# Moving PSUM copies between two activations of a group, and one more rest for a batch's first expert block

## The chip, the cores and the metric

The kernel runs on one core of one Trainium2 chip. The metric is the device time of one execution in microseconds (us), the median of several runs. Before the change it is 1380.28 us (three runs, 1379.79 to 1381.28).

The engines have these names: PE is TensorE (matmuls, and PEld its weight loads), DVE is VectorE, ACT is ScalarE, POOL is GpSimd, and SP issues most of the transfers. Each engine takes its instructions in its own order and waits on semaphores for the others. On PE, ACT and DVE this kernel fixes that order in the program: the order in which the Python code calls the instructions is the order on the engine.

## What is computed

Attention in which each query keeps only its 32 best keys, and then a mixture-of-experts layer in which each token goes to one of eight experts:

```python
# q, k, v: (8 batches, 8 heads, 576 positions, 64)
scores = q @ k.T / sqrt(64)
kth    = the 32nd largest score of each row
attn   = softmax(where(scores >= kth, scores, -1e9)) @ v
x      = attn laid out as (4608 tokens, 512)

logits = x @ w_gate                      # 8 experts
expert = argmax(logits);  gate_w = softmax(logits)[expert]
h      = relu(x @ w1[expert])            # 512 -> 1024
out    = gate_w * (h @ w2[expert])       # 1024 -> 512
```

All of it is float32.

## The kernel before

The attention runs in 144 groups, 18 for each of the 8 batches. A group is two tiles of 128 query rows by 576 scores. Two heads share one unit of the program ("head pair"; 4 per batch, 32 in all). For each group:

- PE multiplies queries and keys (`sc`), four groups ahead; ACT copies the scores to SBUF (`s`);
- DVE folds the scores (`h`, `l`, `few`, `hl`) and finds the 32nd largest in four rounds (`tops`);
- ACT computes `low` from it and then two Relus, one for each tile, which mark how far a score lies under the threshold (`w`); POOL subtracts them from the scores; ACT takes the exponentials;
- PE transposes the weights of the group before (`wTm`, `wTl`), ACT copies them out of PSUM (`wT`, `wTt`);
- when a head pair is complete, PE multiplies with the values (`po`, in two halves), ACT copies the two halves (`oT`), PE turns them to rows and multiplies with the gate (`px`, in two parts), ACT copies both parts (`xl`), and POOL divides by the softmax sums.

The loop over the groups, cut to what the change concerns. `at_place(name)` lets the work at a head pair's end go one step on, if it waits at that name:

```python
for i, (b, g) in enumerate(work):
    f_of[i + 1] = fold(s_of[i + 1])                    # DVE
    low, nbias, doubts = search(tiles, s_of[i], ...)   # DVE, then low on ACT
    at_place("small")
    w_of[i] = depths(s_of[i], low)                     # ACT: two Relus
    less(s_of.pop(i), w_of[i])                         # POOL: two subtractions
    doubts()
    ...
    at_place("pool")
    at_place("relu")                                   # ACT: oT or xl copies
    at_place("rows")                                   # POOL: rows of x
    ...
    s_of[i + AHEAD], steps = scores(...)               # ACT: two copies of s
    for step in steps: step()
    evacuate()                                         # ACT: copies due for expert blocks
    at_place("turn")
    turns = turning(i - 1)
    next(turns, None)                                  # PE: wTm, ACT: wT
    rest = pieces(part)                                # PE: pieces of an expert block
    next(turns, None)                                  # PE: wTl
    rest = pieces(now - now//2 - part + rest)          # PE: pieces
    weights(tiles, w_of[i], nbias)                     # ACT: two exponentials
    next(turns, None)                                  # ACT: wTt
    evacuate()                                         # ACT: copies due for expert blocks
    multiply(i + AHEAD + 1)                            # PE: sc
    ...
    at_place("products")                               # PE: po or px
    at_place("weights")
    credit = min(credit + pieces(now//2 + rest), ...)  # PE: pieces
```

```python
def depths(s, low):
    w = ...
    for m in range(2):
        nc.scalar.activation(w[:, m, :], s[:, m], AF.Relu, scale=-STEEP, bias=low[:, m:m + 1])
    return w
```

The end of a head pair is a generator; each `next(out_steps)` gives a matmul part or a copy of `outputs`:

```python
def outputs(n, x):
    for j in range(2):
        ...                                   # PE: po
        yield
        nc.scalar.copy(oT[...], po[...])      # ACT
        yield
    ...                                       # PE: px, two parts
    yield
    for to, px in put:
        nc.scalar.copy(to, px)                # ACT: xl, two parts
```

All PSUM tiles of transposes and of `po` and `px` share one pool of two buffers (`bank`), so a new one waits until the copy of the one before last has been made. The score tiles and the tiles of the expert blocks have two buffers each in pools of their own.

The expert blocks (40 of 128 tokens, over loaded weights) are cut into 16 pieces each and laid between the groups by a credit that the program works out when it is built; those that are left over run after the last group. A piece is four matmuls of `ph` (128x128x128) or one of `py`. A block turns its rows first (`xtp`), ACT copies them (`xTs`), and `ph` multiplies them. Usually the block before turns the rows of the next in good time; a batch's first block has to do it itself:

```python
def evacuate(upto=None):
    while due and (upto is None or upto in [kind for kind, _ in due]):
        due.pop(0)[1]()

def block(n, ...):
    if not hasattr(n, "xT"):
        turned(n)                  # PE: xtp; the ACT copy to xTs becomes due
        yield "pause"              # no more pieces at this place of the group
    evacuate("xT")                 # ACT: all copies due, up to xTs
    ...                            # PE: ph, ...
```

Of the kernel before, what the change touches and what calls it, by code (L numbers as in the profile page):

```python
# [35 lines left out]
def kernel(  # L36
# [326 lines left out]

        return low, nbias, doubts

    def depths(s, low):

        w = k.att.tile([P, 2, S], F32, name="w", bufs=1 if k.exact else 3)
        for m in range(2):
            nc.scalar.activation(  # L370
                w[:, m, :], s[:, m, :, :].rearrange("p j k -> p (j k)"), AF.Relu,
                scale=-STEEP, bias=low[:, m:m + 1],
            )
        return w

    def less(s, w):
# [44 lines left out]
    def outputs(n, x):  # L421

        odd = n.u % 2
        oT = oT_of[odd]
        for j in range(2):
            q = slice(j * HF + (0 if odd else ST), (j + 1) * HF + (0 if odd else ST))
            po = bank("po")
            for c in range(NC):
                for h in range(2):
                    r = slice(h * D, (h + 1) * D)  # L430
                    nc.tensor.matmul(po[r, 0:HF], n.v[:, c, r], wT[:, c, h, q], start=(c == 0), stop=False)  # L431
            nc.tensor.matmul(po[:, 0:HF], n.v[:, NC, :], wTt[:, q], start=False, stop=True)
            yield
            nc.scalar.copy(oT[:, j * HF:(j + 1) * HF], po[:, 0:HF])
            yield
        starts = [t * P + (ST if odd else 0) for t in range(NC)] + [0 if odd else SM]
        xw = P + lw
        n.xl = k.small.tile([P, KC, xw], F32, name="xl", bufs=1)
        put = []
        for t0, t1 in ((0, KC - 2), (KC - 2, KC)):  # L440
            px = bank("px")
            for t in range(t0, t1):
                nc.tensor.matmul(
                    px[:, (t - t0) * xw:(t - t0 + 1) * xw], oT[:, starts[t]:starts[t] + P],
                    turn[:, n.u // 2, odd * lw:odd * lw + xw], start=True, stop=True,
                )
            put.append((n.xl[:, t0:t1, :], px[:, 0:(t1 - t0) * xw].rearrange("p (t w) -> p t w", w=xw)))
        yield
        for to, px in put:
            nc.scalar.copy(to, px)  # L450

    def divisors(n):
        rz = rz_of[n.u % 2]
# [215 lines left out]
# [5 lines that stand above are left out]
    def block(n, following=lambda: None, put_off=lambda store: store()):  # L674

        if not hasattr(n, "xT"):
            turned(n)
            yield "pause"
        evacuate("xT")
        hT = k.mlp.tile([P, FT, P], F32, name="hT", bufs=1)  # L680
        for half in range(2):
            while half and "y" in [kind for kind, _ in due]:
                yield "pause"
            ph = k.ps_m.tile([P, FT // 2, P], F32, name="ph", tag="m")
            for f in range(FT // 2):
                fc = half * (FT // 2) + f
                for dt in range(DT):
                    nc.tensor.matmul(  # L688
                        ph[:, f, :], n.w1[:, 0, dt, fc * P:(fc + 1) * P], n.xT[:, dt, :],
                        start=(dt == 0), stop=(dt == DT - 1),  # L690
                    )
                if f == FT // 2 - 1:
                    due.append((f"h{half}", lambda ph=ph, half=half: nc.scalar.activation(  # L693
                        hT[:, half * (FT // 2):(half + 1) * (FT // 2), :], ph, AF.Relu
                    )))
                yield
        evacuate("h0")
        following()
        yield "pause"
        evacuate()  # L700
        py = bank("py") if k.apart else k.ps_m.tile([P, Dm], F32, name="py", tag="m")
        for f in range(FT):
            nc.tensor.matmul(py, hT[:, f, :], n.w2[:, 0, f, :], start=(f == 0), stop=(f == FT - 1))  # L703
            if f < FT - 1:
                yield
        y = k.mlp.tile([P, Dm], F32, name="y")

        def store():
            put = nc.gpsimd.indirect_dma_start(  # L709
                out=out[:, :], out_offset=bass.IndirectOffsetOnAxis(ap=n.x[:, 0, Dm + 1:XW].bitcast(I32), axis=0),  # L710
                in_=y[:, :], in_offset=None, bounds_check=N - 1, oob_is_err=False,
            )
            if not k.exact:
                tc.add_manual_dep(put.ins, k.last_pool.name, AFTER)

        def scaled():
            nc.scalar.activation(y, py, AF.Copy, scale=n.x[:, 0, Dm:Dm + 1])  # L717
            put_off(store)

        due.append(("y", scaled))  # L720
        yield "last"
# [13 lines left out]
    with fast:  # L735
# [68 lines left out]
        def ending(b, u):  # L804

            nonlocal left
            n = unit[b * U + u]
            if u == 0:
                x_of[b] = k.xp.tile([P, KC, XW], F32, name="x")
                in_turn(token_ids(x_of[b][:, :, Dm + 1].bitcast(I32), b))  # L810
                lg_of[b] = k.small.tile([P, KC, E], F32, name="lg")
            x, lg = x_of[b], lg_of[b]
            out_steps = outputs(n, x)
            yield "products"
            next(out_steps)
            if u % 2 == 0:
                yield "relu"
                next(out_steps)
            yield "small"
            div = divisors(n)  # L820
            aside.append(div)
            if u % 2:
                yield "relu"
                next(out_steps)
            yield "products"
            next(out_steps)
            if b * U + u + 2 < len(units):
                load_values(unit[b * U + u + 2])
            yield "relu"
            next(out_steps)  # L830
            yield "products"
            next(out_steps)
            yield "relu"
            next(out_steps, None)
            yield "rows"
            through(div)
            logits(n, lg)
            rows(n, x)
            if u < U - 1:
                return  # L840
            yield "small"
            r = choice(lg)
            aside.append(r.steps)
            yield "weights"
            yield "turn"
            through(r.steps)
            nc.scalar.activation(lg, lg, AF.Exp)
            yield "products"
            ranks(r)
            yield "small"  # L850
            steps = places(r, x)
            aside.append(steps)
            yield "relu"
            nc.scalar.copy(run, r.run)
            yield "pool"
            through(steps)
            scatters.extend(scattering(r, x))
            if b == B - 1:
                scatter(KC)
                slot_i = k.small.tile([1, 2, NSLOT], I32, name="slot_i")  # L860
                through(table(slot_i, SURE, False))
                firsts = [(slot_i[0:1, 0, j:j + 1], slot_i[0:1, 1, j:j + 1]) for j in range(SURE)]
                ready = load_rows(SimpleNamespace(), firsts[0][1], True)
            new = LAST - SURE if b == B - 1 else new_of[b]
            if new:
                slot_i = slot_last if b == B - 1 else k.small.tile([1, 2, NSLOT], I32, name="slot_i")
                steps = table(slot_i, new, b == B - 1)
                aside.append(steps)
                yield "weights"
                yield "pool"  # L870
                yield "weights"
                yield "pool"
                through(steps)
                coming.extend((slot_i[0:1, 0, j:j + 1], slot_i[0:1, 1, j:j + 1]) for j in range(new))
            if b == B - 1:
                spare.extend(coming[ALWAYS - SURE:])
                del coming[ALWAYS - SURE:]
                assert len(loaded) == 2 and not waiting
                fill_up()
                coming[0:0] = [(firsts[0][0], ready)] + [(expert, (piece,)) for expert, piece in firsts[1:]]  # L880
                scatter(0)
# [10 lines left out]
        got_of, s_of, f_of, w_of = {}, {}, {}, {}  # L892
# [16 lines left out]
        def loop():  # L909
# [9 lines left out]
            for i, (b, g) in enumerate(work):  # L919
# [10 lines left out]
                    then = lambda: fold_on(f_of[i + 1])  # L930
                low, nbias, doubts = search(tiles, s_of[i], f_of.pop(i), then)
                at_place("small")
                w_of[i] = depths(s_of[i], low)
                less(s_of.pop(i), w_of[i])
                doubts()
                put_stores()
                scatter(1)
                at_place("pool")
                at_place("relu")
                at_place("rows")  # L940
                at = i % per_batch
                if at == FIRST and b:
# [180 lines left out]
```

## Time and profile before

| | busy us | share of the span | instructions |
|---|---|---|---|
| PE | 1242.7 | 90% | 7538 |
| DVE | 1097.6 | 80% | 4655 |
| ACT | 919.9 | 67% | 2049 |
| POOL | 649.9 | 47% | 805 |

The span of the profiled execution is 1378.2 us. The page shows the busy share of each engine in 40 slices of 34.5 us; a digit is tenths, and 9 means 90% or more. The row PEclk is the clock that TensorE was granted, in tenths of full speed. A group in the list of groups is named by its line in the program, its engine, its operation and its tiles (out<-in); the mean length of one follows. The groups that the change moves:

| what | count | mean ns |
|---|---|---|
| Relu of one tile (`w<-s,low`, ACT) | 288 | 768 |
| copy of half the outputs (`oT<-po`, ACT) | 64 | 395 |
| copy of a part of the rows (`xl<-px`, ACT) | 64 | 453 |
| copy of a block's turned rows (`xTs<-xtp`, ACT) | 40 | 608 |
| subtraction of one tile (`w<-s,w`, POOL) | 288 | 1434 |

A wait is shown as the idle time of an engine before an instruction, with the instruction that ended it: "ph <- ACT xTs" means that PE stood idle before `ph` until ACT had written `xTs`. A row of the timeline has the start, the length, the engine, the line, the operation, its tiles and how many equal ones were merged; a bracket at its end gives the idle time before it and its releaser. PE counts a float32 matmul as two passes, so its counts there are twice those of the program.

### The profile page before, as it was taken

To read this page: it belongs to the slowest core of one execution; us is meant where nothing else is said; L and a number is where in the kernel's file an instruction comes from. 1 tells how busy PE (TensorE), PEld (TensorE's weight loads), DVE (VectorE), ACT (ScalarE), POOL (GpSimd) and SP (SyncE) were. 2 spreads that over 40 slices of the span, in tenths; PEclk is the share of its full clock that TensorE was granted. 3 is DMA by queue.
4 is the path that set the end of the run, shared out by engine and by line. 5 is a ranking of instruction groups with operands and counts; after the bars stand their busy time and mean duration, and the time that the engine had idled before them with its cause. 6 is when DMAs were issued, how large, how long until landed. Compare 5 with 4: busy or idle time off the path is not lost. (4 is left out here: it accounts for less than half of the span.)

```text
span 1378.2 us, 24231 instructions
## 1 busy us (share of the span) xinstructions
PE 1242.7 (90%) x7538; PEld 847.1 (61%) x7538; DVE 1097.6 (80%) x4655; ACT 919.9 (67%) x2049; POOL 649.9 (47%) x805
## 2 busy tenths in 40 slices
PE   5776777776799999999999999999999999999995
PEld 3444444444466666766766666767676677776773
DVE  8999999999999999999999999999999820000000
ACT  4788777777788888888777788887777821111110
POOL 3454547546645666466555565675556621000000
PEclk9878787888899999999999999999999999999998
DMA  2000011001483267327645474358552859999880
GB/s 82 29 29 29 28 36 55 29 29 36 162 295 127 106 213 277 132 78 247 246 167 173 149 274 161 109 169 302 187 174 66 315 181 354 387 319 330 302 322 18
DMA packets 102219, 231.66 MB, mean 168 GB/s; under 512 B 5182, under 2 KB 25918, under 8 KB 102080
## 3 DMA queue, kind: packets, MB, share of 16 engines
q1 hardware_dynamic: 95328, 209.76, 43.2%
q0 software_dynamic: 6464, 19.97, 4.0%
q8 instruction: 61, 1.00, 0.3%
q14 instruction: 78, 0.64, 0.1%
q10 hardware_dynamic: 288, 0.30, 0.1%
HBM read 208.72 MB, written 22.33 MB: 168 GB/s over the span
## 5 line engine op out<-in xcount | busy, mean ns | idle before, releaser
L379 POOL TENSOR_TENSOR w<-s,w 128x576 f32<-128x576 f32 x288 | 407.2, 1434 | 451.8 <-ACT w L370 451.7
L688 PE MATMUL ph<-xTs,w 128*128 128x128 f32 x2560 | 307.6, 276 | 6.0 <-ACT xTs L665 6.0
L688 PEld LDWEIGHTS ph<-xTs,w 128*128 128x128 f32 x2560 | 298.3, 192 | 23.2 <-issue 14.9
L703 PE MATMUL py<-w,hT 128*128 128x512 f32 x640 | 292.0, 596 | 0.0
L338 DVE MAX8 tops<-scr 128x8 f32<-128x168 f32 x864 | 248.3, 319 | 0.1
L276 PE MATMUL sc<-qkb 64*128 64x288 f32 (+1 forms) x1280 | 224.1, 476 | 9.6 <-ACT s L283 5.2
L387 ACT ACTIVATE w<-w,nbias 128x576 f32<-128x576 f32 x288 | 224.8, 799 | 2.7 <-POOL w L379 2.5
L370 ACT ACTIVATE w<-s,low 128x576 f32<-128x576 f32 x288 | 207.6, 768 | 4.7
L398 PE MATMUL wTm<-turn,w 128*128 128x128 f32 x1152 | 175.2, 291 | 34.5 <-ACT xl L450 21.1
L398 PEld LDWEIGHTS wTm<-turn,w 128*128 128x128 f32 x1152 | 140.2, 149 | 84.0 <-ACT xl L450 23.5
L1002 DVE CAST any_i<-pd 1x1 int32<-1x1 f32 x1 | 0.1, 146 | 236.0 <-PE pd L1000 236.0
L703 PEld LDWEIGHTS py<-w,hT 128*128 128x128 f32 x640 | 114.6, 190 | 116.9 <-issue 115.6
L345 DVE MATCH_REPLACE8 scr<-tops,scr 128x168 f32<-128x168 f32 x576 | 177.9, 314 | 0.0
L283 ACT COPY s<-sc 128x576 f32<-128x576 f32 x288 | 169.9, 645 | 11.3 <-PE sc L276 10.7
L404 ACT COPY wT<-wTm 128x512 f32<-128x512 f32 x256 | 139.9, 609 | 39.4 <-PE wTm L398 39.2
L276 PEld LDWEIGHTS sc<-qkb 64*128 64x128 f32 (+1 forms) x1280 | 119.2, 197 | 73.2 <-issue 26.0
L431 PE MATMUL po<-wT,vb 128*64 128x288 f32 x1024 | 154.8, 450 | 0.4 <-ACT wTt L419 0.4
L709 POOL DMA_INDIRECT out_dram<-y,xg x40 | 40.6, 1015 | 212.1 <-ACT y L717 199.8
L329 DVE MAX8 few<-l 128x8 f32<-128x288 f32 x288 | 128.0, 445 | 0.0
L431 PEld LDWEIGHTS po<-wT,vb 128*64 128x64 f32 x1024 | 74.7, 151 | 77.2 <-issue 26.1
L693 ACT ACTIVATE hT<-ph 128x512 f32<-128x512 f32 x80 | 48.8, 609 | 108.2 <-PE ph L688 108.1
L290 DVE TENSOR_TENSOR h<-s 128x576 f32<-128x576 f32 x144 | 112.5, 781 | 4.4 <-ACT s L283 4.4
(116 smaller groups left out, 1444.0 us busy)
## 6 DMA issues: line engine op xcount, KB each, us to landing
w<-in_moe_w_dram SPq DMA_DIRECT2D x80, 2048.0 KB, 9.8
qkb<-in_qk_dram SPq DMA_DIRECT2D x31, 608.0 KB, 4.2
xg<-x_rows SPq DMA_DIRECT2D x40, 257.0 KB, 9.8
vb<-in_v_dram SPq DMA_DIRECT2D x32, 320.0 KB, 3.2
x_rows<-blank SPq DMA_DIRECT2D x5, 257.0 KB, 13.8
x_rows<-blank POOLq DMA_DIRECT2D x4, 257.0 KB, 8.7
x_rows<-x,posi POOLq DMA_INDIRECT x40, 3.0
out_dram<-y,xg POOLq DMA_INDIRECT x40, 6.1
```

The costliest lines, as they stand in the source:

```text
L276: nc.tensor.matmul(ps[rows, j, 0:HF], n.q[d, cols], n.k[d, keys], start=True, stop=True)
L283: lambda m=m, ps=ps: nc.scalar.copy(s[:, m, :, :], ps[:, :, 0:HF]) for m, ps in enumerate(got)
L338: nc.vector.max(out=tops[:, m, r * 8:(r + 1) * 8], in_=src[m])
L345: nc.vector.match_replace(out=scr[:, m, :], in_to_replace=tops[:, m, r * 8:(r + 1) * 8], in_values=src[m], imm_value=NEG,)
L370: nc.scalar.activation(w[:, m, :], s[:, m, :, :].rearrange("p j k -> p (j k)"), AF.Relu, scale=-STEEP, bias=low[:, m:m + 1],)
L379: k.last_pool = in_turn(nc.gpsimd.tensor_tensor(w[:, m, :], s[:, m, :, :].rearrange("p j k -> p (j k)"), w[:, m, :], op=ALU.subtract)).ins
L387: nc.scalar.activation(w[:, m, :], w[:, m, :], AF.Exp, scale=scale, bias=nbias[:, m:m + 1], accum_out=n.z[:, c:c + 1])
L398: nc.tensor.transpose(pm[:, c * P:(c + 1) * P], w[:, m, first:first + P], ident)
L404: nc.scalar.copy(wT[:, :, m, q], pm4)
L431: nc.tensor.matmul(po[r, 0:HF], n.v[:, c, r], wT[:, c, h, q], start=(c == 0), stop=False)
L688: nc.tensor.matmul(ph[:, f, :], n.w1[:, 0, dt, fc * P:(fc + 1) * P], n.xT[:, dt, :], start=(dt == 0), stop=(dt == DT - 1),)
L703: nc.tensor.matmul(py, hT[:, f, :], n.w2[:, 0, f, :], start=(f == 0), stop=(f == FT - 1))
```

## The change

The copies of `oT` and the first of the two copies of `xl` are made between the two Relus of a group instead of behind both; the second copy of `xl` keeps its place behind them. This is to let the outputs leave PSUM earlier, so that the two shared buffers come free sooner for the transposes that follow, while POOL can begin its first subtraction as before.

A batch's first expert block rests at one place more after its rows were turned, so that it begins only when ScalarE has copied them out of PSUM, and PE goes on with the score products of the group meanwhile.

```diff
-    def depths(s, low):
+    def depths(s, low, between=lambda: None):
         w = ...
         for m in range(2):
             nc.scalar.activation(
                 w[:, m, :], s[:, m, :, :].rearrange("p j k -> p (j k)"), AF.Relu,
                 scale=-STEEP, bias=low[:, m:m + 1],
             )
+            if m == 0:
+                between()
         return w
...
         yield
         for to, px in put:
             nc.scalar.copy(to, px)
+            yield
...
         if not hasattr(n, "xT"):
             turned(n)
             yield "pause"
+            yield "pause"
         evacuate("xT")
...
             next(out_steps)
             yield "relu"
-            next(out_steps, None)
+            next(out_steps)
+            yield "behind"
+            next(out_steps)
             yield "rows"
...
-                w_of[i] = depths(s_of[i], low)
+                w_of[i] = depths(s_of[i], low, lambda: at_place("relu"))
                 less(s_of.pop(i), w_of[i])
                 doubts()
                 put_stores()
                 scatter(1)
                 at_place("pool")
-                at_place("relu")
+                at_place("behind")
                 at_place("rows")
```

## The prediction, before the changed kernel was run

> **What bounds the kernel now.** I read the slices first, because averages over the span mix stages with different limits.
>
> ```profile
> PE   5776777776799999999999999999999999999995
> ...
> DVE  8999999999999999999999999999999820000000
> ...
> PEclk9878787888899999999999999999999999999998
> ```
>
> The reader is to see two borders. VectorE is full from the start to about slice 32; TensorE becomes full at slice 11, 380 us, where the first expert blocks enter between the attention groups, and stays full to the end. Cut at these borders, the table of stretches (us, then busy time of TensorE, weight loads, VectorE, ScalarE, GpSimd) reads:
>
> ```profile
> 0.00:380.00 380.00, 275.95 (x1429) 166.12 (x1430) 372.82 (x1614) 288.34 (x651) 200.97 (x268) 0.83 0.16 50
> 380.00:1110.00 730.00, 714.48 (x4640) 496.09 (x4640) 716.84 (x2996) 588.98 (x1324) 422.14 (x506) 1.00 0.52 187
> 1110.00:1362.00 252.00, 251.40 (x1468) 184.82 (x1468) 7.61 (x43) 41.86 (x74) 25.81 (x30) 1.00 0.84 301
> ```
>
> Until 380 us VectorE's top-32 search is the bound (373 of 380 us; TensorE only 276). From 380 to 1110 us both look full; after that only expert blocks run, and TensorE has 0.6 us idle in 252. Which of the two leads in the middle? VectorE's own waits in the whole attention part are few (4.4 us for the score copies), but its group period is 7.02 us where nothing disturbs it and 7.75 us on average after group 54, though its work per group is the same. TensorE has a fixed list of instructions, and its waits in the window 390 to 1115 us are short:
>
> ```profile
> PE ph L688 <- ACT xTs L665: 5.3, 5, 1.1
> PE wTl L411 <- ACT wT L404: 3.8, 11, 0.7
> PE wTm L398 <- ACT oT L434: 2.9, 3, 1.0
> PE wTm L398 <- ACT xl L450: 1.3, 1, 1.3
> ```
>
> So from 380 us on **TensorE is the bound**: some 966 us busy in 982. I read the time as 380 us of VectorE, then TensorE's list plus its idle time (some 16 us), then 16 us of closing. A VectorE stall after 380 us costs only if TensorE comes to wait for it; I timed the gap between the end of a group's exponentials and the start of its transposes on TensorE, and it never falls under 2.2 us in the groups from 54 to 141. A ScalarE copy counts only if TensorE waits for it.
>
> **What the Trainium skill says.** "PSUM — Partial Sum Buffer", section "Engine vs sequencer instructions", says that ScalarE's queue is strictly first in, first out and that matmuls start in program order. The trace agrees: ScalarE sat idle 44.0 us in 48 waits before the output copies (oT), with the other work queued behind each. "SBUF — State Buffer", section "Who interferes with whom", says that a VectorE instruction with two SBUF inputs and a GpSimd instruction that reads SBUF lock each other out for a whole instruction. The trace agrees: the fold into `few` takes 0.45 us at the median, but 1.51 us when it starts while GpSimd subtracts. These stalls, worked out as what the four fold instructions of each group take over the fastest tenth of their kind, are some 34 us; I take them as the other channel by which a moved Relu can act.
>
> **Part 1: the second Relu behind the output copy.** No instruction is added or removed; the order of the built program shows equal counts on all engines. Four copies per head pair (2 oT of 0.40 us, 2 xl of 0.45 us), 128 in all, stood behind both Relus (1.44 us a pair, so about 0.7 us each). Now oT and the first xl stand between them. Where the matmul is done already, ScalarE's total is the same and the copy comes 0.7 us earlier. Where ScalarE waits for the matmul (48 of 64 oT, 15 xl), the copy cannot come earlier; the second Relu no longer fills the wait, and everything behind it (s, wT, exponentials) slips by the smaller of the wait and 0.67 us.
>
> What slips matters where TensorE waits for the copy of wT: its next transpose (wTl) needs the bank. For each output group after 380 us I took the slip, took off any time that ScalarE waits for TensorE before wT anyway, and compared it with the distance from the end of the first wT copy to the start of wTl. Most have slack of 0.7 to 1.5 us; tight ones have 0.12 or 0.34 us. The positive remainders sum to 4.8 us, of which 1.8 fall in five groups that part 2 also touches (counted there). **Loss: 3.0 us.** Gain: the three waits for oT (2.9 us) lose 0.67 us each, but in those groups wTl follows with a slack of 0.1 us, so nearly all comes back as a wait there; the one xl wait gives perhaps 0.2 us. **Gain: 0.5 us.**
>
> **Part 2: the second rest of a batch's first block.** It touches six places (380, 514, 649, 797, 932, 1080 us). The built order shows it: before, wTl, two or three pieces of ph (8 or 12 matmuls, which the trace counts as 16 or 24 passes), sc; after, wTl, sc, then all of ph. On TensorE and ScalarE before, at 514 us (start, length):
>
> ```profile
> 513.16 0.27 PE L411 MATMUL wTl<-turn,w 128*128 128x128 f32 x1
> 514.49 2.05 PE L688 MATMUL ph<-xTs,w 128*128 128x128 f32 x16 [1.06 <-ACT xTs L665]
> 516.47 1.24 PE L276 MATMUL sc<-qkb 64*128 64x288 f32 x8
> ```
>
> ```profile
> 512.27 1.11 ACT L404 COPY wT<-wTm 128x512 f32<-128x512 f32 x2
> 513.23 0.73 ACT L717 ACTIVATE y<-py,xg 128x512 f32<-128x512 f32 x1
> 513.81 0.63 ACT L665 COPY xTs<-xtp 128x512 f32<-128x512 f32 x1
> 514.27 0.84 ACT L387 ACTIVATE w<-w,nbias 128x576 f32<-128x576 f32 x1
> ...
> 515.95 0.26 ACT L354 ACTIVATE low<-tops 128x2 f32<-128x2 f32 x1
> ```
>
> The aim is to put sc into the idle 1.06 us. But the copy of xTs moves too: it is no longer forced before the exponentials; it is emitted behind them and behind wTt. These take 515.95 - 514.27 = 1.68 us. So y starts at 513.23 + 1.68 = 514.91, xTs ends 1.21 us later at 516.12, and ph starts at 516.17. TensorE ends wTl at 513.43 and sc (1.17) at 514.60, then idles 1.57 us: 0.51 more than before. With part 1 these groups slip by 0.62 us as well (oT waits 0.62 to 1.02 there): wTl starts 0.28 later, xTs lands at 516.79, idle is 0.28 + 1.91 = 2.19 us against 1.06. So 1.1 us is lost at each of five places, and about 1.0 at 380 us, where there is no y and the slip is 0.36. **Loss: 6.6 us.**
>
> **Before 380 us.** TensorE's waits cost nothing there; VectorE stalls do. If oT starts at time t after `low`, the second subtraction now ends at t + 0.40 (copy) + 0.72 (Relu) + 1.43 = t + 2.55 us. The fold into few comes 5.7 to 6.1 us after `low`. Only where t is over 3.0 do they meet: six groups, up to 0.5 us each. **Loss: 1.4 us.**
>
> **Sum:** 3.0 - 0.5 + 6.6 + 1.4 = +10.5 us: 1380.3 becomes 1390.8. I take 1390.
>
> **Rivals.** (a) The change does what it is for: the xTs waits go (5.3 + 0.7 us), the waits for oT and xl after 380 us shrink by 2 to 3 us. For it: these are the longest entries in TensorE's waits. Against it: the place of the xTs copy in ScalarE's order. Then some 1372. (b) VectorE becomes the bound in the middle too: in the groups where ScalarE waits 1 to 2.6 us for an output, the second subtraction runs over the folds, and by the same arithmetic VectorE loses about 4.5 us in a dense batch (I walked through batch 5), against TensorE's some 3. It leads only if it eats the 2.2 us of slack; then 1393 to 1397. (c) Nothing moves: TensorE regains the idle time elsewhere, because a late TensorE finds its later copies ready. The waits outside xTs come to some 9 us after 390 us, so it can regain a part; then 1381 to 1385. The other way round, the split subtraction leaves a gap in which a fold can slip through; that lowers stalls, but after 380 us it isn't on the path.
>
> **Range and chances.** The losses come from shifts of half a microsecond at known places, so the size is uncertain but bounded: the whole of TensorE's idle time is 16 us, and (a) and (b) span 1372 to 1397. Most weight lies between (c) and (b): 1381 to 1399. A move of 2% is 27.6 us, more than any of these makes; faster by 2% 0.01, within 0.98, slower by 2% 0.01.
>
> **What would show it.** In the changed profile: TensorE's wait for xTs up from 6.0 to about 10 us in six waits, each behind sc; TensorE's wait of wTl for wT after 390 us up from 3.8 to about 7; oT idle on ScalarE up from 44 us to 60 or more, with the second Relu behind it; waits for oT on TensorE near nothing; the end of VectorE's search later by some 8 to 10 us; the stretch after it unchanged. I am wrong if xTs is ready when sc ends, if TensorE had slack that its busy time hides, or if fold stalls before 380 us change by several us.

## The result and the profile after

The changed kernel takes 1421.94 us (median of five runs) against 1379.79 us before: a ratio of 1.0299, with a 95% interval of 1.0285 to 1.0313. It is 42 us slower; the prediction said 10.5, within 1381 to 1399.

Cut at the first `ph`, at the start of the last fold `h` of the search and at the end of the last `py`, the profile of the changed kernel reads, with the columns length, then busy time of TensorE, weight loads, VectorE, ScalarE and GpSimd, then the granted clock, the DMA share and GB/s:

```profile
0.00:393.70 393.70, 275.75 (x1436) 162.11 (x1436) 384.05 (x1620) 288.88 (x655) 207.12 (x268) 0.86 0.17 55
393.70:1128.00 734.30, 701.76 (x4501) 489.20 (x4501) 706.27 (x2930) 565.25 (x1275) 434.18 (x490) 0.99 0.52 179
1128.00:1404.70 276.70, 273.83 (x1603) 199.29 (x1602) 21.96 (x105) 60.58 (x119) 38.35 (x47) 1.00 0.80 283
```

and for the kernel before, cut in the same way:

```profile
0.00:379.80 379.80, 275.80 (x1428) 165.97 (x1428) 372.62 (x1612) 288.14 (x651) 200.97 (x268) 0.83 0.16 50
379.80:1086.00 706.20, 693.26 (x4510) 481.95 (x4511) 702.85 (x2937) 570.70 (x1281) 409.51 (x490) 1.00 0.53 188
1086.00:1362.70 276.70, 273.48 (x1602) 199.15 (x1601) 21.80 (x106) 60.35 (x119) 38.44 (x47) 1.00 0.81 288
```

The first stretch is 13.9 us longer, the second 28.1; the third is as long as before, as the prediction said. In the second TensorE's idle time (length less busy) went from 12.9 to 32.5 us. The other 8.5 us are busy time that grew, most of it in `ph`: 313.8 us over the span instead of 307.6, for as many matmuls. In this stretch the granted clock is half of full speed for 3.4 us at five places (from 393.7, 619.0, 677.0, 912.5 and 970.6 us), each less than 1 us after TensorE had stood idle for 1.1 to 2.5 us. Sixteen passes of `ph` behind an idle time of 2.48 us with such a drop, and behind one of 2.49 us without it:

```profile
618.70 3.35 PE L692 MATMUL ph<-xTs,w 128*128 128x128 f32 x16
477.89 1.95 PE L692 MATMUL ph<-xTs,w 128*128 128x128 f32 x16
```

In the kernel before, this stretch has no such place. Why the clock drops at some of these idle times and not at others stays open. What TensorE waited for, from its waits in the window 390 to 1150 us of the changed kernel (total, times, longest):

```profile
PE wTl L413 <- ACT wT L406: 13.1, 23, 1.1
PE ph L692 <- ACT xTs L668: 9.8, 6, 1.7
PE wTm L400 <- ACT oT L436: 8.1, 4, 2.5
PE py L707 <- ACT hT L697: 2.5, 5, 0.6
```

The wait for xTs is what the prediction said (about 10 us in six waits). The one for wT is twice what it said, and the one for oT should have gone. The waits of VectorE hold a line that the prediction has nothing for:

```profile
DVE pos L528 <- ACT run L860: 20.4, 8, 3.4
DVE h L290 <- ACT s L283: 12.7, 11, 2.0
```

and in the kernel before:

```profile
DVE h L290 <- ACT s L283: 4.4, 4, 1.6
DVE pos L525 <- ACT run L854: 1.8, 1, 1.8
```

`pos` is the first of six small instructions that turn a batch's routing into places, once for each of the eight batches. Before, VectorE waited for `run` only after the last search. The timeline of VectorE in the changed kernel at such a place:

```profile
462.08 0.56 DVE L338 MAX8 tops<-scr 128x8 f32<-128x168 f32 x2
466.00 0.20 DVE L528 TENSOR_TENSOR pos<-rank,oh 128x40 f32<-128x40 f32 x1 [3.36 <-ACT run L860]
466.12 0.19 DVE L530 TENSOR_REDUCE den<-lg 128x5 f32<-128x40 f32 x1
...
466.97 1.82 DVE L290 TENSOR_TENSOR h<-s 128x576 f32<-128x576 f32 x1
```

The busiest engine of this stage stands still for 3.4 us between one search and the next fold. The fold behind it then takes 1.82 us instead of its usual 0.73; it starts while GpSimd subtracts (from 465.39 to about 468.2 us by GpSimd's timeline). In the kernel before, the same instruction of the same batch sits inside the following search and waits for nothing:

```profile
451.58 0.32 DVE L338 MAX8 tops<-scr 128x8 f32<-128x168 f32 x1
451.83 0.18 DVE L525 TENSOR_TENSOR pos<-rank,oh 128x40 f32<-128x40 f32 x1
451.93 0.32 DVE L338 MAX8 tops<-scr 128x8 f32<-128x168 f32 x1
```

The diff tells why, once it is read for everything that waits at the place "relu", and not for the output copies alone. The end of a batch uses that name too:

```python
yield "small"
steps = places(r, x)          # six VectorE steps, laid into the next search
aside.append(steps)
yield "relu"
nc.scalar.copy(run, r.run)    # ScalarE
yield "pool"
through(steps)                # whatever of them is left: now, in one block
```

In the loop the place "pool" stood ahead of "relu", so a step that went through "relu" in one group reached "pool" in the next, after a whole search. Since the change "relu" lies inside the Relus, ahead of "pool": both are passed in one group, and the six steps are emitted in one block before the next search can take them in. The block begins with a read of the PSUM tile from which ScalarE is still to copy `run`, behind `low` and the first Relu.

### The profile page after: what moved, and what is told of

Read it like the earlier page. It is cut to its first block, busy times and chain, and to the rows that moved or that the text cites. A ratio compares the mean times of both kernels' runs of the same rounds, so it can differ in the third digit from the quotient of the medians.

```text
span 1420.3 us, 24230 instructions
## 1 busy us (share of the span) xinstructions
PE 1251.5 (88%) x7538; PEld 850.7 (60%) x7538; DVE 1112.6 (78%) x4655; ACT 915.4 (64%) x2049; POOL 680.6 (48%) x805
## 5 line engine op out<-in xcount | busy, mean ns | idle before, releaser
L381 POOL TENSOR_TENSOR w<-s,w 128x576 f32<-128x576 f32 x288 | 413.8, 1448 | 451.9 <-ACT w L370 410.4
L692 PE MATMUL ph<-xTs,w 128*128 128x128 f32 x2560 | 313.8, 280 | 9.8 <-ACT xTs L668 9.8
L692 PEld LDWEIGHTS ph<-xTs,w 128*128 128x128 f32 x2560 | 305.4, 196 | 26.1 <-issue 12.6
L276 PE MATMUL sc<-qkb 64*128 64x288 f32 (+1 forms) x1280 | 219.2, 467 | 9.8 <-ACT s L283 5.2
L370 ACT ACTIVATE w<-s,low 128x576 f32<-128x576 f32 x288 | 218.6, 774 | 4.7
L400 PE MATMUL wTm<-turn,w 128*128 128x128 f32 x1152 | 171.3, 282 | 27.6 <-ACT oT L436 12.6
L400 PEld LDWEIGHTS wTm<-turn,w 128*128 128x128 f32 x1152 | 133.9, 144 | 79.3 <-ACT oT L436 26.9
L433 PE MATMUL po<-wT,vb 128*64 128x288 f32 x1024 | 159.3, 460 | 0.4 <-ACT wTt L421 0.4
L290 DVE TENSOR_TENSOR h<-s 128x576 f32<-128x576 f32 x144 | 126.2, 876 | 12.7 <-ACT s L283 12.7
L413 PE MATMUL wTl<-turn,w 128*128 128x128 f32 x128 | 40.6, 317 | 93.8 <-ACT wT L406 93.8
```

Source lines behind the costliest of these rows:

```text
L276: nc.tensor.matmul(ps[rows, j, 0:HF], n.q[d, cols], n.k[d, keys], start=True, stop=True)
L370: nc.scalar.activation(w[:, m, :], s[:, m, :, :].rearrange("p j k -> p (j k)"), AF.Relu, scale=-STEEP, bias=low[:, m:m + 1],)
L381: k.last_pool = in_turn(nc.gpsimd.tensor_tensor(w[:, m, :], s[:, m, :, :].rearrange("p j k -> p (j k)"), w[:, m, :], op=ALU.subtract)).ins
L400: nc.tensor.transpose(pm[:, c * P:(c + 1) * P], w[:, m, first:first + P], ident)
L692: nc.tensor.matmul(ph[:, f, :], n.w1[:, 0, dt, fc * P:(fc + 1) * P], n.xT[:, dt, :], start=(dt == 0), stop=(dt == DT - 1),)
```

## Experiments

Theory R: the routing's block is the larger part of the loss. Rival W: it is the work that now stands behind ScalarE's wait for TensorE. Ratios and gains or losses against the kernel before are against its time on the same chip.

### The parts one by one

**Routing copy back behind the Relus**, all else as changed:

```diff
-            yield "relu"
+            yield "behind"
             nc.scalar.copy(run, r.run)
```

> The changed kernel, but the copy of the routing counters (run, 128x8) waits at the place behind both Relus, as before; all else as changed. Theory R (the shared place name pulled the routing's six VectorE steps into one block right behind a search, where VectorE stands until that copy): VectorE's wait for run goes from 20.4 to about 2 us and the time falls by some 30 us, to about 1392. Rival W (the output copies between the Relus make ScalarE late and lock VectorE's folds): falls by 5 us or less, to about 1417.

Measured: 1404.19 us, ratio 1.0168 (1.0151 to 1.0185). The wait for `run` is back at 1.8 us. It recovers some 18 us, between the two theories: R is right in kind, but something else costs more than R left for it.

**Only the routing copy moved**, on the kernel before:

```diff
-            yield "relu"
+            yield "run"
             nc.scalar.copy(run, r.run)
...
-                w_of[i] = depths(s_of[i], low)
+                w_of[i] = depths(s_of[i], low, lambda: at_place("run"))
```

> The kernel before, with only the copy of the routing counters moved between the Relus, and so the routing's steps one group earlier; output copies and the rest as before. Theory R: slower by about 30 us, 1410, with VectorE waiting some 20 us for run. Rival W: slower by 8 us at most.

Measured: 1400.24 us, ratio 1.0145 (1.0128 to 1.0162), 19.4 us slower. From the waits of VectorE over the whole span:

```profile
DVE pos L527 <- ACT run L856: 18.9, 8, 3.1
```

and from those of TensorE in the window 390 to 1130 us:

```profile
PE wTm L400 <- ACT oT L436: 11.0, 6, 3.1
```

One tiny copy, with the steps that it pulls along, gives nearly half of the whole loss. The second view tells how a stall of VectorE reaches TensorE: `low` comes late, the oT copy stands behind it on ScalarE, and TensorE waits for the bank. The 8.1 us of this wait in the changed kernel are of the same kind: they are 1.2 us where the routing copy is put back.

**Only the second rest**, on the kernel before (one more `yield "pause"`):

> The kernel before, with only the second rest of a batch's first block. By the prediction's arithmetic without the slip of the Relus: 0.5 us at each of six places, 1383. Rival (the rest hides the wait as meant): 1374. TensorE's wait for xTs about 9 us instead of 6.

Measured: 1382.15 us, ratio 1.0013 (1.0004 to 1.0022). The timeline of TensorE at the first such place after 500 us:

```profile
513.85 1.24 PE L276 MATMUL sc<-qkb 64*128 64x288 f32 x8
516.65 4.73 PE L689 MATMUL ph<-xTs,w 128*128 128x128 f32 x40 [1.56 <-ACT xTs L665]
```

The idle time after sc is 1.56 us; the prediction had worked out 1.57. The wait for xTs in all is 8.9 us.

**Only the output copies between the Relus** (the changed kernel with the routing copy behind them and a single rest):

> The changed kernel with the routing copy behind the Relus and a single rest: only the output copies between the Relus. Theory R with the prediction's sum for this part: 3 - 0.5 + 1.4 us and up to 3 us more, 1384 to 1388. Rival W: 1410.

Measured: 1397.21 us, ratio 1.0123 (1.0106 to 1.0140): 16.4 us, four times what the prediction had for this part. The three stretches, cut as above:

```profile
0.00:386.30 386.30, 270.28 (x1428) 158.06 (x1428) 379.36 (x1620) 287.90 (x651) 208.31 (x268) 0.86 0.16 52
386.30:1103.90 717.60, 696.24 (x4512) 482.85 (x4513) 709.17 (x2930) 567.85 (x1281) 434.69 (x490) 1.00 0.51 183
1103.90:1380.30 276.40, 273.53 (x1601) 198.97 (x1599) 21.60 (x105) 60.21 (x118) 38.27 (x47) 1.00 0.80 291
```

6.5 us are lost before the first block, all of them in VectorE's busy time (372.6 to 379.4), and 11.4 in the middle, where TensorE's idle time goes from 12.9 to 21.4 us. ScalarE's wait for oT tells how:

```profile
ACT oT L436 <- PE po L434: 89.4, 58, 2.6
```

In the kernel before it was:

```profile
ACT oT L434 <- PE po L432: 44.0, 48, 2.6
```

The run with only the routing copy put back is this one with the second rest besides, and takes 7.0 us more. Its waits for xTs and for s, and then those of this run:

```profile
PE ph L692 <- ACT xTs L668: 9.8, 6, 1.7
DVE h L290 <- ACT s L283: 14.6, 12, 2.6
```

```profile
PE ph L691 <- ACT xTs L668: 6.8, 6, 1.2
DVE h L290 <- ACT s L283: 9.1, 12, 1.8
```

### Two checks of the routing and of the rest

**The routing copy between the Relus, the step after it in the following group**:

```diff
             yield "relu"
             nc.scalar.copy(run, r.run)
+            yield "rows"
             yield "pool"
```

> The changed kernel; the copy of the routing counters stays between the Relus, but the routing's next step on VectorE is held back to the following group, as it was before. If the loss in the routing comes from the step's six instructions standing in one block that has to wait for ScalarE: 1403 to 1405, as with the copy behind the Relus, and VectorE's wait for run back near 2 us. If the place of the copy itself costs: it stays near 1420.

Measured: 1402.20 us, ratio 1.0151 (1.0135 to 1.0168), as with the copy behind the Relus (1404.19); VectorE's wait for `run` is back at 1.8 us. So the place of the copy costs nothing that shows; the block of steps that it pulled along does.

**The rest, with xTs copied ahead of the exponentials**, on the kernel before:

```diff
             turned(n)
             yield "pause"
+            yield "pause"
...
+                evacuate("xT")
                 weights(tiles, w_of[i], nbias)
                 next(turns, None)
```

> The kernel before with the second rest, and the due copies up to xTs made ahead of the exponentials instead of behind them. If TensorE sets the time after 380 us: the idle time before ph is covered by sc at six places, TensorE's wait for xTs goes from 6 us to near nothing, and the time falls by about 6 us, to 1374. If VectorE sets it: 1380.

Measured: 1374.88 us, ratio 0.9960 (0.9945 to 0.9974), 5.5 us faster than the kernel before. The timeline of TensorE at the same place as above:

```profile
512.49 1.24 PE L276 MATMUL sc<-qkb 64*128 64x288 f32 x8
513.66 4.73 PE L689 MATMUL ph<-xTs,w 128*128 128x128 f32 x40
```

ph follows sc at once, and TensorE's wait for xTs is gone. TensorE's idle time is worth about its full length here: 5 waits of 1.06 us and one of 0.7, and 5.5 us of gain. VectorE ends its last search 5.0 us sooner too (1093.4 instead of 1098.4 us), with the same work: a part of its busy time gives way when TensorE is early, so an engine that is never idle for long need not be the one that sets the time.

### How much stands behind the wait

**Output copies ahead of both Relus** (from the kernel before; the routing copy stays behind):

```diff
+                at_place("relu")
                 w_of[i] = depths(s_of[i], low)
```

> The kernel before with the output copies ahead of both Relus (the routing copy stays behind). If the work that stands behind ScalarE's wait is the cost, it doubles: ScalarE's wait for oT goes to 120 us or more and the time to 1400 to 1415. If it is the subtraction on GpSimd being cut in two, which puts its second half over VectorE's folds: the two subtractions are together again, and the time is 1388 or less.

Measured: 1451.43 us, ratio 1.0516 (1.0498 to 1.0533), more than either reading had. ScalarE's wait for oT is 125.5 us. In the window 390 to 1180 us TensorE waits for wT:

```profile
PE wTl L411 <- ACT wT L404: 40.2, 50, 2.2
```

The first stretch, in which VectorE is the bound, grows from 379.8 to 404.0 us, and nearly all of that is VectorE's busy time (372.62 before):

```profile
0.00:404.00 404.00, 285.54 (x1429) 174.94 (x1429) 396.73 (x1612) 286.44 (x651) 209.00 (x268) 0.82 0.14 45
```

The fold into few takes 35.4 us of it instead of 25.2, the fold into hl 29.0 instead of 22.8, for 51 instructions each. Over the whole span 65 of the 144 folds into few start while GpSimd subtracts; before it was 22. So a late Relu also costs by way of the subtraction that it releases late.

The two subtractions are together again here, and it is far slower: a loss does not need them cut in two, it is enough to hold work behind the wait. This does not show how much of the 16.4 us of the copies alone comes by the wait for wT and how much by late subtractions. The cost isn't linear: with one Relu held behind 96 copies (64 of oT, 32 of xl) it is 16.4 us, with two behind 128 copies 71.

**Output copies behind the copies of s**, which have 1.2 us to fill the wait with:

```diff
-                at_place("relu")
-                at_place("rows")
...
                     for step in steps:
                         step()
+                at_place("relu")
+                at_place("rows")
                 evacuate()
```

> The kernel before with the output copies moved later, behind the two copies of s (1.2 us). If the cost of the change is that ScalarE stands waiting for TensorE with its other work behind it: ScalarE's wait for oT falls from 44 us to under 15, and the time stays or falls, 1374 to 1381. If an early release of the two shared PSUM buffers is what counts: slower, 1386 or more, with TensorE's waits for oT and xl grown.

Measured: 1382.52 us, ratio 1.0016 (1.0009 to 1.0023). The wait shrank as expected, from 44.0 to 10.4 us, but TensorE's wait for the bank grew after 390 us:

```profile
PE wTm L398 <- ACT oT L434: 11.6, 19, 1.6
```

It was 2.9 us. The time lies between the two readings. What ScalarE no longer waits and what TensorE waits more for the bank about cancel; that both count fits this, but the run does not part them. None of the places tried for the output copies was better than that of the kernel before.

**Only oT between the Relus, and only the first xl:** both from the run with only the output copies moved, the first with both xl copies at "behind", the second with the oT copies there.

> Only the oT copies between the Relus; both xl copies, the routing copy and the rest as before. If the cost follows what ScalarE adds in idle time with the Relu behind it (with both kinds moved, oT added 45 us of such idle time and xl 7): most of the 16 us are here, 1391 to 1395. If the cost comes from the xl copies, by way of GpSimd's row products that follow them: 1385 or less.

> Only the first xl copy between the Relus; oT behind them as before. By the idle time: 1381 to 1384. By way of GpSimd's row products: 1390 or more.

Measured: oT alone 1395.11 us, ratio 1.0098 (1.0082 to 1.0113), with 86.4 us of waits for oT on ScalarE; xl alone 1382.32 us, 1.0014 (1.0007 to 1.0020). The cost goes with the idle time that each adds, and a move of the first xl copy, with GpSimd's row products behind it, costs 1.5 us in all.

**The rest with xTs first, and the output copies between the two copies of s** (the part of the edit that places the copies):

```diff
-                    for step in steps:
-                        step()
+                    steps[0]()
+                    at_place("relu")
+                    steps[1]()
```

> The kernel before with the rest and xTs ahead of the exponentials (1374.9), and the output copies between the two copies of s, so that one s copy of 0.6 us fills part of ScalarE's wait. If the freed ScalarE time counts: 1371 to 1374. If TensorE's waits for oT grow as much as those for wT shrink: 1375 to 1377.

Measured: 1375.76 us, ratio 0.9958 (0.9945 to 0.9972): the same as without the move, within the intervals. ScalarE's wait for oT is 17.8 us, TensorE's for the bank after 390 us 5.2 us, against 41.3 and 1.8 without the move: as above, the two about cancel.

## Why the prediction was wrong, point by point

- **The bound.** That TensorE's idle time sets the time after 380 us holds where it was tested: the gain of 5.5 us in the run with xTs first is close to the 6.0 us of waiting that it takes away. "A VectorE stall costs only if TensorE comes to wait for it" holds too, but the 2.2 us of slack was taken as enough for all that would come, and the stalls in the routing are 3.4 us and more at once. Nor was the size "bounded" by the 16 us of idle time that TensorE had: a new order makes new idle time, 19.6 us more in the middle stretch alone, and 13.9 us were lost ahead of it. A chance of 0.01 for slower by 2% was far too small.
- **The step that failed first: "the order of the built program shows equal counts on all engines", and with it the parts list.** Counts were compared, and TensorE's and ScalarE's order, but the prediction has no term for VectorE's order. There the routing's six instructions moved from inside a search to a block in front of one. It costs some 18 us within the change and 19.4 by itself.
- **The second: the loss of part 1, 3.0 - 0.5 + 1.4 = 3.9 us, measured 16.4.** The mechanism is the predicted one as far as the runs part it (ScalarE waits with the second Relu behind it, wT and s slip), and its size was wrong. The middle was 2.5 us and measured 11.4: the slip was taken as none where ScalarE had not waited before, but a copy that stands 0.7 us earlier can come too early for its matmul; waits rose from 48 to 58, by 45 us in all, and TensorE's wait for wT from 3.8 to 11.9 us in the run with the copies alone. VectorE's busy time grows there too, by 6.3 us, and its wait for s from 4.4 to 9.1 us over the span, with all of the increase after 670 us; how much of the 11.4 comes by this way was not tested.
- **Of this, the stretch before 380 us: 1.4 us, measured 6.5.** Only the fold into few was counted; it took 27.0 us instead of 25.2 (with one instruction more), but h took 42.2 instead of 38.9 us for 52 instructions, and single small instructions of the routing were longer too (one on its counters 1.38 us, against 0.16 on average before). The 1.51 us that the prediction gives for a fold into few under a subtraction is the longest of its 22 cases; they run from 0.51 to 1.51, 0.96 at the median.
- **Part 2 was right in its size, in part by luck.** Without the slip the idle time is 1.56 us, worked out 1.57; but the six places make 3 us by this arithmetic, and 1.4 were lost. With the slip 6.6 us, measured as the difference of 1404.19 (copies and rest) and 1397.21 (copies alone): 7.0. But the idle time before ph is 1.72 us at five of the places in the changed kernel, not 2.19, and of the 7.0 us TensorE's longer wait for xTs shows 3.0. What grew besides is VectorE's wait for s, by 5.5 us, which the prediction does not have.
- **Rivals.** (a), the xTs wait hidden, fell by the order on ScalarE, as said against it; put that order right and the part of it about xTs comes true. (b), VectorE leading in the middle, is nearest: with the routing moved, its stalls pass through the late `low` to TensorE. (c) fell.
- **The sum.** Alone, routing 19.4, copies 16.4 and rest 1.4 make 37.2 of the 42 us; the 5.6 us that the rest costs more together with the copies make up the remainder, to within about a microsecond.

## What to carry to other kernels

Where the program's order is given by named places, moving a place moves everyone who waits there, and the order of two places decides in which round a step that passes both will land; look at the order on each engine, above all the busiest one, and not only at what the diff was meant for. A copy that has to wait for another engine belongs behind work that doesn't, up to the point where its buffer is missed; moving it earlier won nothing here where it waited already, and held up what stood behind it. A wait is hidden only if what ends it is issued in time: the rest needed the copy of xTs ahead of the exponentials before it paid.

## What the runs showed that was not expected

The cost of a wait in an in-order queue grew much faster than the work behind it: 0.7 us of Relu behind 96 copies cost 16.4 us, 1.4 us behind 128 copies 71, and 24.2 of these 71 fell where VectorE is the bound, in its busy time. And six routing instructions, some 1.1 us of busy time per batch, cost 2.4 us per batch by their place alone.
